# Cluster masks of a routing attention on four 32-row groups of TensorE instead of two 64-row groups

## The chip, the cores and the metric

The kernel runs on one core of one Trainium2 chip. The metric is the device time of one execution in microseconds; the lower, the better. The kernel before takes 916.72 us (median of three runs).

## The reference

Two blocks follow each other. The first is an attention in which a query sees only the keys of its own cluster; the second is an MLP mixer over tokens and channels. The change touches the attention alone.

```python
B, H, S, D = 4, 8, 768, 64          # batch, heads, sequence, head size; 16 clusters per head
q_assign = argmax(q_n @ c_n.T)      # nearest of 16 normalised centroids of the head
k_assign = argmax(k_n @ c_n.T)
mask   = q_assign[:, :, :, None] == k_assign[:, :, None, :]
scores = where(mask, 0.125 * q @ k.T, -1e9)
attn   = softmax(scores)
x      = (attn @ v), heads side by side: (B, S, 512)

h   = relu(x.T @ w_tok1) @ w_tok2   # over tokens
u   = x + h.T
out = u + relu(u @ w_ch1) @ w_ch2   # over channels
```

## The kernel before

TensorE makes the mask itself. Each query and key has a one-hot vector of its cluster. The keys' one-hots are scaled by a large number BIG and lowered by it, so that a product of a query's one-hot with a key's is 0 where the clusters agree and -BIG where they don't. This product goes into PSUM first, the scores are added on top, and the exponential turns what is masked into 0.

Two heads are treated at once, as a pair; there are 16 pairs (4 batches, 4 pairs of heads). In every tile that is contracted, head 0 of the pair has partitions 0-63 and head 1 has partitions 64-127. One pair has 6 steps, each of two chunks of 128 keys against half of the queries (384), so the attention has 96 steps. The matmuls of head 0 and head 1 use separate row groups of the array.

The clusters are found one pair ahead. After the similarities are turned, a comparison with the maximum writes the one-hots: 16 elements wide at the front of each head's 64, the rest zero from the start. TensorE transposes them, and ScalarE copies them out of PSUM with scale and offset.

```python
# const / rsmall: the one-hots, [tokens, q or k, chunk, 2 heads x 64], zeroed once
ohs = [rsmall.tile([P, 2, NJ, P], BF16, name=f"oh{i}", bufs=1) for i in range(2)]

def route(g, a0=0, a1=2):
    ...  # sc: similarities of 16 clusters; mx: their maximum
    oh = ohs[g % 2][:, a0:a1].rearrange("p a j (h x) -> p (a j) h x", h=2)[:, :, :, 0:C]
    nc.vector.tensor_tensor(
        out=oh, in0=sc..., in1=mx...to_broadcast([P, NR // 2, 2, C]), op=ALU.is_ge)

def route_turn(g, a):
    po = ps_w.tile([P, NJ, P], BF16, tag="w", name="po")
    for j in range(NJ):
        nc.tensor.transpose(out=po[:, j], in_=oh[:, a, j], identity=identb)
    ...  # a == 0 (queries): plain copy to ohT[:, 0]
    ...  # a == 1 (keys): ohT[:, 1] = BIG * po - BIG, and its sum into cells[:, g]

def scores(m):
    g, qh, j0 = split(m)
    st = state[g]
    js = slice(HJ * qh, HJ * qh + HJ)
    scs = [ps_sc.tile([P, 2, 512], F32, name="sc") for _ in range(2)]   # two banks each
    for src, start in ((st["ohT"], True), (st["T"], False)):            # mask, then scores
        for i in range(2):                                              # chunk of keys
            for h in range(2):                                          # head
                rows = slice(h * D, (h + 1) * D)
                nc.tensor.matmul(
                    scs[i][:, h, 0:HS], lhsT=src[rows, 1, j0 + i], rhs=src[rows, 0, js],
                    start=start, stop=not start,
                )
    for i in range(2):
        ex = work.tile([P, 2, HS], F32, name="ex")
        nc.scalar.activation(out=ex, in_=scs[i][:, :, 0:HS], func=ACT.Exp, scale=SM_SCALE)

def values(m):            # two steps later: 4 float32 matmuls, 128 rows x 64 columns
    ...
def half_sums(hi):        # den: column sums, 128 rows x 32 columns
    ...
def half_turn(hi):        # px: transposes, 128 x 128
    ...
```

The order on TensorE within one step m is: scores(m) (masks, then scores), values(m - 2), and then, depending on the step, what the next pair's routing needs (pr, po) or the end of a half (den, px). At the very end, the sum over cells is compared with the number of tokens, to find ties between clusters; in case of a tie a general version of the program runs, which isn't the case for these inputs.

Of the kernel before, what the change touches and what calls it, by code (L numbers as in the profile page):

```python
# [16 lines left out]
B, H, S, D = 4, 8, 768, 64  # L17
C = 16
P = 128
# [8 lines left out]
HS = HJ * P  # L28
WMAX = 512
NQ = 4  # L30
QP = P // NQ
# [15 lines left out]
def kernel(  # L47
# [29 lines left out]
    nc = tc.nc  # L77
# [39 lines left out]
    ohs = [rsmall.tile([P, 2, NJ, P], BF16, name=f"oh{i}", bufs=1) for i in range(2)]  # L117
# [185 lines left out]
    def route(g, a0=0, a1=2):  # L303

        st = state[g]
        NR = (a1 - a0) * NJ * 2
        sc = rsmall.tile([P, NR, C], F32, name="sim")
        nc.vector.transpose(  # L310
            out=sc.rearrange("p n c -> p (n c)"), in_=st.pop("pr").rearrange("p a j r -> p (a j r)")
        )
        mx = rsmall.tile([P, NR], F32, name="mx")
        nc.vector.reduce_max(out=mx, in_=sc, axis=AX.X)
        oh = ohs[g % 2][:, a0:a1].rearrange("p a j (h x) -> p (a j) h x", h=2)[:, :, :, 0:C]
        nc.vector.tensor_tensor(
            out=oh, in0=sc.rearrange("p (n h) c -> p n h c", h=2),
            in1=mx.rearrange("p (n h) -> p n h", h=2).unsqueeze(3).to_broadcast([P, NR // 2, 2, C]),
            op=ALU.is_ge,
        )  # L320

# [25 lines left out]
    def split(m):  # L347

        g, s = divmod(m, GROUPS)
        return g, s // (GROUPS // 2), 2 * (s % (GROUPS // 2))  # L350

    def scores(m):
        g, qh, j0 = split(m)
        st = state[g]
        js = slice(HJ * qh, HJ * qh + HJ)
        scs = [ps_sc.tile([P, 2, 512], F32, name="sc") for _ in range(2)]
        for src, start in ((st["ohT"], True), (st["T"], False)):
            for i in range(2):
                for h in range(2):
                    rows = slice(h * D, (h + 1) * D)  # L360
                    nc.tensor.matmul(  # L361
                        scs[i][:, h, 0:HS], lhsT=src[rows, 1, j0 + i], rhs=src[rows, 0, js],
                        start=start, stop=not start,
                    )
        for i in range(2):
            ex = work.tile([P, 2, HS], F32, name="ex")
            nc.scalar.activation(out=ex, in_=scs[i][:, :, 0:HS], func=ACT.Exp, scale=SM_SCALE)  # L367
            st["ex", qh, j0 + i] = ex
# [297 lines left out]
    def fits():  # L666

        inside = const.tile([P, 3, 2 * NPAIR * 2 * HJ], F32, name="inside")
        good = const.tile([P, 3], F32, name="good")
        flat = rcps.rearrange("p n h j -> p (n h j)")  # L670
        for i, (limit, op) in enumerate(((LIMIT, ALU.is_le), (1.0 / LIMIT, ALU.is_ge))):
            nc.vector.tensor_scalar(
                out=inside[:, i], in0=flat, scalar1=limit, scalar2=None, op0=op
            )
            nc.vector.tensor_reduce(out=good[:, i : i + 1], in_=inside[:, i], axis=AX.X, op=ALU.min)

        nc.vector.tensor_scalar(
            out=inside[:, 2, 0:NPAIR], in0=cells, scalar1=1.0 / BIG, scalar2=float(S),
            op0=ALU.mult, op1=ALU.add,
        )  # L680
        nc.vector.reduce_sum(out=good[:, 2:3], in_=inside[:, 2, 0:NPAIR], axis=AX.X)
        pn = ps_w.tile([1, 3], F32, tag="w", name="pn")
        nc.tensor.matmul(pn, lhsT=ones[:, 0:1], rhs=good, start=True, stop=True)
        count = const.tile([1, 3], I32, name="count")
        nc.vector.tensor_copy(out=count[:, 0:2], in_=pn[:, 0:2])
        nc.vector.tensor_scalar(
            out=count[:, 2:3], in0=pn[:, 2:3], scalar1=float(B * H * S), scalar2=float(P),
            op0=ALU.is_equal, op1=ALU.mult,
        )
        loaded = [  # L690
            nc.values_load(count[0:1, i : i + 1], min_val=0, max_val=P) for i in range(3)
        ]
        return loaded[0] + loaded[1] + loaded[2]


    def begin():
# [23 lines left out]
        route_products(0, 1, 2)  # L720
        turn(0, (0,))
        route(0, 1, 2)
        keep_warm(1)
        route_products(0, 0, 1)
        keep_warm(2)
        route_turn(0, 1)
        route(0, 0, 1)
        keep_warm(1)
        route_turn(0, 0)
# [15 lines left out]
    for m in range(last + 5):  # L745
        g, s = divmod(m, GROUPS)
# [4 lines left out]
        if m < last:  # L751
            scores(m)
# [4 lines left out]
        if g < NPAIR - 1:  # L757
            if s == 0:
                turn(g + 1)
            elif s == 1:  # L760
                route_products(g + 1)
            elif s == 2:
                route(g + 1)
            elif s == 3:
                route_turn(g + 1, 1)
            elif s == 4:
                route_turn(g + 1, 0)
# [35 lines left out]
    for b in range(B):  # L803
        for part in range(2):
            for i in range(3):
                ch1_chunk(part, i)
                for _ in range(2):
                    if beside:
                        beside.pop(0)()
            for i in range(3):  # L810
                ch2_chunk(b, part, i)
                if part == 1 and i < 2 and b + 1 < B:
                    turn_u(b + 1, i)
            if b == 0 and part == 0:
                both = fits()
# [213 lines left out]
```

## Time and profile before

| What | Before |
|---|---|
| time, median of 3 runs | 916.72 us (915.32 to 916.98) |
| profiled execution, span | 913.0 us |
| granted TensorE clock, mean | 0.995 |
| TensorE busy | 897.8 us |
| VectorE busy | 506.1 us |
| ScalarE busy | 306.9 us |
| attention steps | from 14.3 us (first mask) to 369.6 us (first token matmul) |
| MLP | from 369.6 us on |

A line of a group names the line of the kernel, the engine and the operation, the tile written and the tiles read, partitions x elements and type, and the count; then the busy time in us and the mean length of one in ns; then the time that the engine was idle just before. For a matmul, "64*128" is rows times columns of the array, and the next "64x384" is what streams through it. PE is TensorE's matmuls and PEld its weight loads. Matmuls are pipelined: several overlap, and a length from start to end is more than what one adds to the time. A line of the timeline gives start, length, engine, line, operation, tiles, shapes and count, merged for neighbours of one kind. A line of windows gives a stretch and then the busy time of PE, PEld, VectorE, ScalarE and GpSimd in it with the number of instructions, then the clock, the share of the transfers and GB/s.

### The profile page before, as it was taken

To read this page: it belongs to the slowest core of one execution; us is meant where nothing else is said; L and a number is where in the kernel's file an instruction comes from. 1 tells how busy PE (TensorE), PEld (TensorE's weight loads), DVE (VectorE), ACT (ScalarE), POOL (GpSimd) and SP (SyncE) were. 2 spreads that over 40 slices of the span, in tenths; PEclk is the share of its full clock that TensorE was granted. 3 is DMA by queue.
4 is the path that set the end of the run, shared out by engine and by line. 5 is a ranking of instruction groups with operands and counts; after the bars stand their busy time and mean duration, and the time that the engine had idled before them with its cause. 6 is when DMAs were issued, how large, how long until landed. Compare 5 with 4: busy or idle time off the path is not lost.

```text
span 913.0 us, 11598 instructions
## 1 busy us (share of the span) xinstructions
PE 897.8 (98%) x4594; PEld 527.4 (58%) x4594; DVE 506.1 (55%) x851; ACT 306.9 (34%) x515; POOL 48.4 (5%) x40
## 2 busy tenths in 40 slices
PE   7999999999999999999999899999999999999997
PEld 3444444444444444444458668677686876858676
DVE  6778787878787765358554244333443334433342
ACT  3656565656565555222120021211212012130210
POOL 1001000101010100123000000000000000000000
PEclk9999999999999999999999999999999999999999
DMA  9543535353434200122000001000010000100001
GB/s 163 117 100 69 93 87 97 83 98 81 95 85 70 88 1 1 47 92 70 0 1 0 1 0 47 24 1 1 0 47 24 0 1 7 52 12 1 1 12 61
DMA packets 112830, 41.76 MB, mean 46 GB/s; under 512 B 101632, under 2 KB 105728, under 8 KB 112768
## 3 DMA queue, kind: packets, MB, share of 16 engines
q1 hardware_dynamic: 109632, 40.55, 18.9%
q10 hardware_dynamic: 3136, 0.39, 0.3%
q8 instruction: 38, 0.62, 0.3%
q14 instruction: 24, 0.20, 0.1%
HBM read 34.64 MB, written 6.29 MB: 45 GB/s over the span
## 4 chain that ended last, share of the span: by engine, by line
PE 98%; DMA 1%; DVE 0%; issue 0%; ACT 0%
PE sc L361 18%; PE av L390 15%; PE pX L596 14%; PE pX L647 14%; PE pZ L647 7%; PE pZ L596 7%; PE ph L463 5%; PE pu L472 5%; PE pY L647 3%; PE pY L596 3%; PE px L425 2%; PE po L334 2%; PE pr L296 1%; PE den L406 1%; PE pt L535 1%; DMA qk<-in_k_dram 1%
## 5 line engine op out<-in xcount | busy, mean ns | idle before, releaser
L367 ACT ACTIVATE ex<-sc 128x768 f32<-128x768 f32 x192 | 145.1, 808 | 116.6 <-PE sc L361 116.6
L380 DVE TENSOR_TENSOR sum<-sum,ex 128x768 f32<-128x768 f32 x128 | 132.8, 1037 | 31.1 <-ACT ex L367 22.6
L390 PE MATMUL av<-ex,va 128*64 128x384 f32 x768 | 145.1, 499 | 0.0
L361 PE MATMUL sc<-qkT 64*128 64x384 f32 x768 | 139.5, 482 | 0.0
L390 PEld LDWEIGHTS av<-ex,va 128*64 128x64 f32 x768 | 46.6, 136 | 86.5 <-issue 82.7
L361 PEld LDWEIGHTS sc<-qkT 64*128 64x128 f32 x768 | 70.5, 187 | 31.4
L596 PE MATMUL pX<-uT,wc 128*128 128x384 f32 x192 | 68.8, 495 | 1.6 <-issue 1.6
L604 ACT COPY p<-pX 128x384 f32<-128x384 f32 x24 | 11.4, 475 | 153.0 <-PE pX L596 153.0
L596 PEld LDWEIGHTS pX<-uT,wc 128*128 128x128 f32 x192 | 36.7, 193 | 26.7 <-issue 3.3
L361 PE MATMUL sc<-ohT 64*128 64x384 bf16 x384 | 48.2, 328 | 1.3 <-DVE ohT L337 0.6
L222 POOL TENSOR_TENSOR wc<-wT,wup 128x512 int32<-128x512 int32 x24 | 35.2, 1466 | 257.7 <-DVE wT L215 149.1
L431 DVE TENSOR_TENSOR x<-px,rcps 128x384 f32<-128x384 f32 x32 | 17.8, 557 | 47.9 <-PE px L425 46.8
L463 PE MATMUL ph<-x,wt 128*128 128x512 f32 x96 | 42.1, 594 | 0.0
L472 PE MATMUL pu<-h,wt 128*128 128x512 f32 x96 | 42.0, 592 | 0.0
L489 DVE TENSOR_TENSOR x<-pX,x 128x256 f32<-128x256 f32 x24 | 10.2, 423 | 53.0 <-PE pX L647 53.0
L489 DVE TENSOR_TENSOR c<-pZ,u 128x384 f32<-128x384 f32 x24 | 13.4, 557 | 46.9 <-PE pZ L596 46.9
L647 PE MATMUL pX<-w2s,hA 128*128 128x256 f32 x144 | 35.4, 382 | 0.5 <-DVE x L489 0.5
L489 DVE TENSOR_TENSOR hA<-pY,p 128x384 f32<-128x384 f32 x24 | 13.4, 557 | 40.4 <-PE pY L596 40.4
L647 PE MATMUL pX<-wc,hA 128*128 128x256 f32 x144 | 35.0, 379 | 0.0
L647 PE MATMUL pZ<-w2s,hS 128*128 128x256 f32 x144 | 35.0, 379 | 0.0
L647 PE MATMUL pZ<-wc,hS 128*128 128x256 f32 x144 | 35.0, 379 | 0.0
L647 PE MATMUL pY<-wc,hA 128*128 128x256 f32 x144 | 35.0, 379 | 0.0
(115 smaller groups left out, 1216.7 us busy)
## 6 DMA issues: line engine op xcount, KB each, us to landing
raw<-in_moe_w_ch_dram SPq DMA_DIRECT2D x24, 512.0 KB, 4.1
qk<-in_k_dram SPq DMA_DIRECT2D x64, 96.0 KB, 4.7
va<-in_v_dram SPq DMA_DIRECT2D x16, 384.0 KB, 3.3
out_dram<-x SPq DMA_DIRECT2D x24, 256.0 KB, 2.0
qk<-in_q_dram SPq DMA_DIRECT2D x60, 96.0 KB, 3.5
raw<-in_moe_w_tok_dram SPq DMA_DIRECT2D x3, 512.0 KB, 5.8
raw<-in_moe_w_tok_dram SPq DMA_DIRECT2D x4, 384.0 KB, 3.9
qk<-in_q_dram ACTq DMA_DIRECT2D x4, 96.0 KB, 4.3
```

Of the source, the lines that this page charges most:

```text
L222: nc.gpsimd.tensor_tensor(out=dst.bitcast(I32), in0=T, in1=up, op=ALU.add)
L334: nc.tensor.transpose(out=po[:, j], in_=oh[:, a, j], identity=identb)
L361: nc.tensor.matmul(scs[i][:, h, 0:HS], lhsT=src[rows, 1, j0 + i], rhs=src[rows, 0, js], start=start, stop=not start,)
L367: nc.scalar.activation(out=ex, in_=scs[i][:, :, 0:HS], func=ACT.Exp, scale=SM_SCALE)
L380: nc.vector.tensor_tensor(out=acc, in0=acc, in1=e[i], op=ALU.add)
L390: nc.tensor.matmul(st["av"][h * D : (h + 1) * D], lhsT=st["va"][:, h, j], rhs=ex[:, h], start=(j == 0), stop=(j == NJ - 1),)
L425: nc.tensor.transpose(out=px[:, i], in_=avT[:, i], identity=ident)
L463: nc.tensor.matmul(pf, lhsT=W["tok1"][:, j, t * P : (t + 1) * P], rhs=xs[b][:, j], start=(j == 0), stop=(j == NJ - 1),)
L472: nc.tensor.matmul(pu, lhsT=W["tok2"][:, t, j], rhs=h1s[b][:, t], start=(t == 0), stop=(t == NT - 1))
L489: nc.vector.tensor_tensor(out=dst, in0=a, in1=b, op=ALU.add)
L596: nc.tensor.matmul(psum, lhsT=A[a][:, k, c * P : (c + 1) * P], rhs=R[r][:, k], start=start and k == 0, stop=k == 1, skip_group_check=not s ...
L647: nc.tensor.matmul(psum, lhsT=h2[a][:, k, i * P : (i + 1) * P], rhs=Bw[w][:, 3 * part + k], start=start and k == 0, stop=k == 2, skip_grou ...
```

## The change

A one-hot has 16 elements, and 32 rows are enough to contract it; the mask takes 64 only because head 1 begins at partition 64. The change writes each one-hot twice, to the first 16 of both 32-wide halves of its head. Then the mask of the first chunk of keys uses rows 0-31 and 64-95 (heads 0 and 1), and that of the second chunk rows 32-63 and 96-127, so that the four mask matmuls of a step use four different row groups of 32. The aim is that all four run side by side rather than two and two. The scores stay on two groups of 64 rows. Since every one-hot is there twice, the sum compared at the end is doubled.

```diff
-        oh = ohs[g % 2][:, a0:a1].rearrange("p a j (h x) -> p (a j) h x", h=2)[:, :, :, 0:C]
+        oh = ohs[g % 2][:, a0:a1].rearrange("p a j (h y x) -> p (a j h) y x", h=2, y=2)[:, :, :, 0:C]
         nc.vector.tensor_tensor(
-            out=oh, in0=sc.rearrange("p (n h) c -> p n h c", h=2),
-            in1=mx.rearrange("p (n h) -> p n h", h=2).unsqueeze(3).to_broadcast([P, NR // 2, 2, C]),
+            out=oh, in0=sc.unsqueeze(2).to_broadcast([P, NR, 2, C]),
+            in1=mx.unsqueeze(2).unsqueeze(3).to_broadcast([P, NR, 2, C]),
             op=ALU.is_ge,
         )
@@ scores
-        for src, start in ((st["ohT"], True), (st["T"], False)):
-            for i in range(2):
-                for h in range(2):
-                    rows = slice(h * D, (h + 1) * D)
-                    nc.tensor.matmul(
-                        scs[i][:, h, 0:HS], lhsT=src[rows, 1, j0 + i], rhs=src[rows, 0, js],
-                        start=start, stop=not start,
-                    )
+        for i in range(2):
+            for h in range(2):
+                r = h * D + (i % 2) * QP
+                nc.tensor.matmul(
+                    scs[i][:, h, 0:HS], lhsT=st["ohT"][r : r + QP, 1, j0 + i],
+                    rhs=st["ohT"][r : r + QP, 0, js], start=True, stop=False,
+                )
+        for i in range(2):
+            for h in range(2):
+                rows = slice(h * D, (h + 1) * D)
+                nc.tensor.matmul(
+                    scs[i][:, h, 0:HS], lhsT=st["T"][rows, 1, j0 + i], rhs=st["T"][rows, 0, js],
+                    start=False, stop=True,
+                )
@@ the test for ties
-            out=count[:, 2:3], in0=pn[:, 2:3], scalar1=float(B * H * S), scalar2=float(P),
+            out=count[:, 2:3], in0=pn[:, 2:3], scalar1=float(2 * B * H * S), scalar2=float(P),
```

## The prediction

> **What bounds the kernel now.** I read the page first: the busy shares, then the chain that ended last.
>
> ```profile
> PE 897.8 (98%) x4594; PEld 527.4 (58%) x4594; DVE 506.1 (55%) x851; ACT 306.9 (34%) x515; POOL 48.4 (5%) x40
> ...
> PE 98%; DMA 1%; DVE 0%; issue 0%; ACT 0%
> PE sc L361 18%; PE av L390 15%; PE pX L596 14%; PE pX L647 14%; PE pZ L647 7%; PE pZ L596 7%; PE ph L463 5%; PE pu L472 5%; PE pY L647 3%; PE pY L596 3%; PE px L425 2%; PE po L334 2%; PE pr L296 1%; PE den L406 1%; PE pt L535 1%; DMA qk<-in_k_dram 1%
> ```
>
> The chain is TensorE from end to end, and the changed line, L361, has 18% of it. But L361 holds both the mask and the scores, so next I read the groups by shape:
>
> ```profile
> L361 PE MATMUL sc<-qkT 64*128 64x384 f32 x768 | 139.5, 482 | 0.0
> L361 PEld LDWEIGHTS sc<-qkT 64*128 64x128 f32 x768 | 70.5, 187 | 31.4
> L361 PE MATMUL sc<-ohT 64*128 64x384 bf16 x384 | 48.2, 328 | 1.3 <-DVE ohT L337 0.6 <-ACT ex L367 0.6
> ```
>
> The mask's 384 matmuls are four in each of 96 steps; the scores' 768 records are eight per step, since a float32 matmul shows as two. Busy time here is a union of overlapping instructions, so what one matmul costs must be read from start to start. That is what the timeline of one step gives (start, length, line, count; the lines come from adjacent and overlapping windows):
>
> ```profile
> 201.48 0.27 PE L425 MATMUL px<-ident,avT 128*128 128x128 f32 x1
> 201.68 0.50 PE L361 MATMUL sc<-ohT 64*128 64x384 bf16 x4
> 202.02 0.49 PE L361 MATMUL sc<-qkT 64*128 64x384 f32 x2
> 202.34 0.48 PE L361 MATMUL sc<-qkT 64*128 64x384 f32 x2
> 203.40 0.54 PE L390 MATMUL av<-ex,va 128*64 128x384 f32 x2
> ```
>
> The four masks occupy 0.34 us (201.68 to 202.02), although each lasts 0.33 us: two heads run side by side on rows 0-63 and 64-127, and the second chunk's pair follows the first. The scores run in pairs 0.32 us apart, and the values begin 1.38 us after the first score, four pairs (1.29) and 0.09 more.
>
> That 0.09 is the key to this case. From the records' start times I took medians over the whole attention stage. Where the shape of the array changes, the next matmul starts late: scores (64 rows x 128 columns) to values (128x64) 412 ns where the pitch is 319, so **+93**; values to mask 418 against 316, **+102**; transposes (128x128) to mask, where the rows alone change, 205 against 109 and 152 against 56, **+96** both times. Mask to scores, today without a change of shape, is 159: no extra. After each change of shape, the second batch also comes late, because no weights could be loaded ahead: bf16 masks 170 against 159 (+11), float32 values of 64 columns 367 against 316 (+51). For float32 weights of 128 columns the case is where the first token matmuls follow the values:
>
> ```profile
> 369.61 0.70 PE L463 MATMUL ph<-x,wt 128*128 128x512 f32 x1
> 370.14 1.02 PE L463 MATMUL ph<-x,wt 128*128 128x512 f32 x2
> 370.57 0.59 PE L463 MATMUL ph<-x,wt 128*128 128x512 f32 x1
> ```
>
> Here the first lasts 0.70 instead of 0.59, and the second starts 0.53 us later where the next takes 0.43: 533 against 429 in the records, **+104**.
>
> **What the Trainium skill says.** "TensorEngine Tiling (Array Packing)", section Key Properties: changing the tiling mode, as opposed to changing only the tile, drains TensorE. The trace agrees: about 96 ns at each of the changes above. "TensorE: Matmul & The Clock Gate", section Part 3, gives 3.07 times for four row tiles of 32; the trace before has no such matmul, but den's four column tiles of 32 start 7 ns apart, so packing by four is seen on columns. The same page, section LDWEIGHTS, puts a load at columns divided by 1.2 GHz whatever the rows: 107 ns for 128 columns, against the 104 ns exposed here.
>
> **The change part by part.**
>
> Removed: the second batch of masks in each step. Today a step goes first mask +3, +170, +3, +159 to the first score, 335 ns. With 32 rows each, the four masks need four different row groups and write four different PSUM banks, so I expect them to start within about 10 ns of each other, and the next batch to be able to start after one pitch with the exposed bf16 load: 170 ns. Alone, that would save 335 - (10 + 170) = 155 ns, or 96 x 0.155 = 14.9 us.
>
> Added: one more change of shape. The scores still contract 64 rows, and now follow 32-row masks. By the row-only change above I add 96 ns: 10 + 170 + 96 = 276 ns to the first score. Then the first score's float32 weights are no longer loaded behind the masks, so the first score pair takes 104 ns more: 322 + 104 = 426. Up to the second score pair, before: 335 + 322 = 657; after: 276 + 426 = 702. That is **+45 ns per step**, 96 x 45 = **+4.3 us**. The change into the mask costs the same as now, since it was a change of shape before.
>
> Added on VectorE: the one-hot comparison writes both copies. It now takes, in the view of this line:
>
> ```profile
> L316 DVE TENSOR_TENSOR oh<-sim,mx x17: 358/557/558, 11.5 to 333.4; 128x384 bf16<-128x384 f32 x15, 128x192 bf16<-128x192 f32 x2
> ```
>
> From 192 to 384 elements is +199 ns, so I estimate 557 + 2 x 199 = 955 ns for the 768 elements to come: 15 x 0.40 = 6.0 us more VectorE, plus 2 x 0.2 at the start. In the stretches of 80 us VectorE has room:
>
> ```profile
> 40.00:120.00 80.00, 80.00 (x591) 35.30 (x591) 62.82 (x94) 46.80 (x72) 8.59 (x6) 1.00 0.46 93
> ```
>
> The third and fourth columns of busy time are VectorE's 62.82 and ScalarE's 46.80 of 80 us, while TensorE has all 80. A group of six steps is 22 us, so 0.4 more is about 2% on VectorE. In the group shown the comparison ended at 202.07 and its transposes began at 204.85: 2.8 us of room, so none of the 6.0 us reaches TensorE. Only the two at the start, before the first mask at 14.26 us, are in a chain (compare, transpose, copy, mask): +0.4 us.
>
> Unchanged: transposes of the one-hots (full 128x128 tiles, zeros or not), copies of ohT, loads, and all of the MLP after 366 us. The count compared at the end doubles at no cost. Sum: 4.3 + 0.4 = +4.7 us on 916.7, giving **921.4 us**.
>
> **Rivals.**
>
> 1. *No drain between 32-row and 64-row tiles.* The extra 96 and 104 ns vanish and the whole 14.9 us come in: 916.7 - 14.9 + 0.4 = 902 us. For it: both are row tilings with all columns, a pair the trace never shows. Against: 128 rows to 64 rows is also a change of rows alone, and it costs the full 96 ns in each of 46 cases. A half-way house, a drain whose weights are loaded ahead, gives 657 - (276 + 322) = 59 ns saved per step, 5.7 us, so 911 us.
> 2. *The four masks don't truly run together* (the four banks or the operand reads limit them to two at a time). Then the mask keeps its 335 ns and both extra terms come on top: about 200 ns x 96 = 19 us, 936 us. For it: nothing in the trace runs four row groups. Against: the skill's 3.07 times, and den on columns.
> 3. *VectorE becomes the bound* by the longer comparison delaying sums and reciprocals, which hold PSUM buffers. It would cost at most the 6.0 us added, so 927 us with my TensorE term. Against: TensorE idles 0 of 80 us there, while VectorE has some 17 us of slack in the same stretch.
>
> **Range and chances.** I give about 78% to the sum above, which the spread of the three runs (915.3 to 917.0) widens to some 919 to 924; 14% to rival 1 or its half-way form; 8% to rivals 2 and 3. I put the range at 911 to 926: it covers the half-way form and part of rival 3. Two per cent is 18.3 us. The best case, 14.9 us, is short of it, so faster by over 2% is nearly out (0.02); slower needs rival 2 in full (0.05); the rest is within (0.93).
>
> **What would show it.** In the timeline after, one step should read: four masks starting within 0.01 us; the first score some 0.28 us after the first mask (0.18 would be rival 1, 0.34 or more rival 2); the second score pair 0.43 after the first (0.32 would mean hidden weights); and the first score's length grown by about 0.1, as with ph. The score's weight loads should start together with the first score, no longer some 0.16 us ahead of it. The comparison should read about 955 ns, x15, with no TensorE idle behind it. The MLP from the first ph to the end should last as before. If the stage grows elsewhere than between masks and second score pair, I am wrong about VectorE; if the drain or load between 32 and 64 rows differs from 96 and 104 ns, the sum moves by 9.6 us per 100 ns.

## The result, and the profile after

The changed kernel takes 921.59 us (median of 6 runs, 919.55 to 924.15), the kernel before 916.04 us in the same comparison. The ratio is 1.0061 with a 95% interval of 1.0041 to 1.0081: some 0.6% slower, within the 2% on either side.

The page of the changed kernel, with the same two parts as before:

```profile
PE 901.8 (98%) x4594; PEld 521.8 (57%) x4594; DVE 512.4 (56%) x851; ACT 306.8 (33%) x515; POOL 48.4 (5%) x40
...
PE 98%; DMA 1%; DVE 0%; issue 0%; ACT 0%
PE sc L368 16%; PE av L397 15%; PE pX L603 14%; PE pX L654 14%; PE pZ L654 7%; PE pZ L603 7%; PE ph L470 5%; PE pu L479 4%; PE pY L654 3%; PE pY L603 3%; PE sc L361 3%; PE px L432 2%; PE po L335 2%; PE den L413 1%; PE pr L296 1%; PE pt L542 1%
```

TensorE is still the whole chain. Masks and scores now have lines of their own, L361 and L368. The groups by shape tell where the time moved:

```profile
L368 PE MATMUL sc<-qkT 64*128 64x384 f32 x768 | 149.8, 508 | 0.0
L368 PEld LDWEIGHTS sc<-qkT 64*128 64x128 f32 x768 | 66.1, 186 | 41.4 <-issue 16.6
L361 PE MATMUL sc<-ohT 32*128 32x384 bf16 x384 | 33.4, 331 | 1.3 <-DVE ohT L338 0.6 <-ACT ex L374 0.6
```

The masks' busy time falls from 48.2 to 33.4 us: the packing works. The scores, which the change doesn't touch, rise from 139.5 to 149.8 us, and their mean length from 482 to 508 ns; their minimum is still 482, but the first pair of each step now takes 587. The weight loads have a new idle time, 16.6 us of issue over 96 waits: they can no longer run ahead of their matmul.

One step in the timeline, the counterpart of the step shown before (again from adjacent and overlapping windows; PEld lines are weight loads):

```profile
204.59 0.27 PE L432 MATMUL px<-ident,avT 128*128 128x128 f32 x1
204.79 0.10 PEld L361 LDWEIGHTS <-ohT 32*128 32x128 bf16 x4 [0.17 <-issue]
204.79 0.34 PE L361 MATMUL sc<-ohT 32*128 32x384 bf16 x4
205.06 0.30 PEld L368 LDWEIGHTS sc<-qkT 64*128 64x128 f32 x4 [0.17 <-issue]
205.06 0.59 PE L368 MATMUL sc<-qkT 64*128 64x384 f32 x2
205.49 0.49 PE L368 MATMUL sc<-qkT 64*128 64x384 f32 x2
206.55 0.54 PE L397 MATMUL av<-ex,va 128*64 128x384 f32 x2
```

All four masks together last 0.34 us, as long as one. But the first score comes 0.27 us after the first mask (0.34 before), not one pitch of 0.16 after it; its weight load starts with it; it lasts 0.59 instead of 0.49; and the second pair follows 0.43 later instead of 0.32. In the records the masks give back 65 ns of a step (336 to 271 from first mask to first score), and the stretch from first score to first value takes 108 ns more (1383 to 1491): +43 ns. A group of six steps, from a first mask to that of the next pair, confirms it: 22.387 us before, 22.643 after, the same to 2 ns in every group from the second on. That is +42.7 ns per step, +4.1 us over 96 steps.

The profiled executions differ by 5.0 us (918.0 against 913.0 us). The rest is at the start: the first mask begins at 14.85 instead of 14.26 us, and the first six steps lose 0.3 us beyond the steady rate. Before the first mask come the last one-hot transposes of the first pair, here in the kernel before and then in the changed one:

```profile
13.10 0.51 PE L334 MATMUL po<-identb,oh 128*128 128x128 bf16 x6
13.38 0.82 PE L335 MATMUL po<-identb,oh 128*128 128x128 bf16 x6
```

They begin 0.28 us later, when the longer comparison has ended, and they take 0.31 us more, at a granted clock of 0.50 instead of 1.00 in these stretches. The 0.3 us are in the second and third step. There the second chunk's masks start 0.70 and 0.25 us after the first chunk's (0.70 and 0.24 before), so that packing gives nothing back, and each of these steps loses 0.2 us instead of 0.04. The MLP takes 543.3 us in the changed kernel and 543.4 in the kernel before.

### The profile page after: what moved, and what is told of

Same layout as the page of the kernel before. It is cut to its first block, busy times and chain, and to the rows that moved or that the text cites. A ratio compares the mean times of both kernels' runs of the same rounds, so it can differ in the third digit from the quotient of the medians.

```text
span 918.0 us, 11598 instructions
## 1 busy us (share of the span) xinstructions
PE 901.8 (98%) x4594; PEld 521.8 (57%) x4594; DVE 512.4 (56%) x851; ACT 306.8 (33%) x515; POOL 48.4 (5%) x40
## 4 chain that ended last, share of the span: by engine, by line
PE 98%; DMA 1%; DVE 0%; issue 0%; ACT 0%
PE sc L368 16%; PE av L397 15%; PE pX L603 14%; PE pX L654 14%; PE pZ L654 7%; PE pZ L603 7%; PE ph L470 5%; PE pu L479 4%; PE pY L654 3%; PE pY L603 3%; PE sc L361 3%; PE px L432 2%; PE po L335 2%; PE den L413 1%; PE pr L296 1%; PE pt L542 1%
## 5 line engine op out<-in xcount | busy, mean ns | idle before, releaser
L368 PE MATMUL sc<-qkT 64*128 64x384 f32 x768 | 149.8, 508 | 0.0
L368 PEld LDWEIGHTS sc<-qkT 64*128 64x128 f32 x768 | 66.1, 186 | 41.4 <-issue 16.6
L654 PE MATMUL pX<-wc,hS 128*128 128x256 f32 x144 | 35.0, 379 | 0.0
L654 PE MATMUL pX<-w2s,hS 128*128 128x256 f32 x144 | 35.0, 379 | 0.0
```

What stands on the lines that cost most here:

```text
L368: nc.tensor.matmul(scs[i][:, h, 0:HS], lhsT=st["T"][rows, 1, j0 + i], rhs=st["T"][rows, 0, js], start=False, stop=True,)
L654: nc.tensor.matmul(psum, lhsT=h2[a][:, k, i * P : (i + 1) * P], rhs=Bw[w][:, 3 * part + k], start=start and k == 0, stop=k == 2, skip_grou ...
```

## The experiments

### Each half of the change alone

**The second copy alone** keeps the masks on 64 rows.

```diff
+        oh = ohs[g % 2][:, a0:a1].rearrange("p a j (h y x) -> p (a j h) y x", h=2, y=2)[:, :, :, 0:C]
 ...
+            out=oh, in0=sc.unsqueeze(2).to_broadcast([P, NR, 2, C]),
+            in1=mx.unsqueeze(2).unsqueeze(3).to_broadcast([P, NR, 2, C]),
 scores(): as before
```

> The second copy alone: the comparison writes both copies as in the changed kernel, but masks run on 64 rows in two batches as before (a mismatch then gives twice -BIG, which the exponential turns into 0 as well); nothing is left out. Theory (VectorE's extra 6 us stay off the path but for the start): a group of six steps takes 22.39 us as before, +0.4 to 0.6 us before the first mask, so 916 to 917 us (ratio 1.0005). Rival (the longer comparison holds up sums or transposes): groups longer than 22.39 us, up to +6 us, 921 us.

Measured: 916.84 against 915.56 us, ratio 1.0005 (0.9998 to 1.0012). The ratio is not that of the two medians, since the executions of both kernels lie near 915.5 and near 917 us and a median falls on one side or the other. From the second group on, a group takes 22.387 us, as before. VectorE's busy time in a stretch of this kernel rises, and TensorE (first busy column) still has every microsecond of it; VectorE is the third:

```profile
40.00:120.00 80.00, 80.00 (x583) 35.19 (x579) 64.52 (x94) 46.31 (x71) 7.59 (x5) 1.00 0.45 92
```

So the longer comparison doesn't reach the path in the steady state. Its share at the start, 0.4 us by the working of the prediction, is smaller than this interval can show. The profiled execution doesn't show it apart either: its first mask comes at 15.24 us, but TensorE ran part of its start at half pace (granted clock 0.91 from 14 to 40 us, against 1.00 in the kernel before).

**The row groups alone** write each one-hot once. The second chunk's rows of the queries' one-hots are then zero, so its mask is left out, and the output isn't the reference's; the instructions on TensorE are those of the changed kernel.

```diff
 route(): as before
 scores():
+                r = h * D + (i % 2) * QP
 ...
+                    scs[i][:, h, 0:HS], lhsT=st["ohT"][r : r + QP, 1, j0 + i],
+                    rhs=st["ohT"][r : r + QP, 0, js], start=True, stop=False,
```

> The four row groups alone: masks as in the changed kernel, but each one-hot is written once, as before. The second chunk of keys in each step then has only zeros in its rows of the queries' one-hots, so its mask is left out. Theory (TensorE pays for one more change of shape per step): the whole loss but the start is there without the longer comparison. From the trace after, 9 + 261 + 427 = 697 ns per step up to the second score pair against 657, +40 ns x 96 = +3.8 us, so about 920 us (ratio 1.004). Rival (VectorE's second copy makes the loss, packing alone pays): the mask's saving without its cost, 902 to 916 us.

Measured: 921.88 against 915.58 us, ratio 1.0060 (1.0045 to 1.0075). The groups from the second on take 22.643 us, exactly those of the changed kernel. So the loss sits in the row groups and the rival is out. By the ratio the loss is 5.5 us (4.1 to 6.9): my 3.8 us is just below this interval, and the steady rate, 4.1 us, at its edge. In the profiled execution a part of the rest is at the start, where TensorE ran the first scores at half pace:

```profile
15.74 2.93 PE L367 MATMUL sc<-qkT 64*128 64x384 f32 x8
```

Eight score records take 2.93 us here and 1.56 later on in the same kernel. Half pace comes without row groups too: in the profiled execution of the second copy alone, with masks on 64 rows, the first eight score records take 2.79 us instead of the usual 1.45. How long it lasts differs between executions; whether the row groups also lengthen it is not shown.

### The change of shape without the packing

Masks contract 32 rows, but both chunks use the same two groups, as two batches. Nothing is gained, and nothing is left out.

```diff
-    rows = slice(h * D, (h + 1) * D)          # mask, 64 rows
+    r = h * D                                 # mask, rows r : r + 32, for both chunks
     ...
```

> The change of shape without the packing: masks of 32 rows, but both chunks on the same two row groups (0-31 and 64-95), one-hots written once; nothing is left out. Theory: a step has the two mask batches of before, then the change of shape and the exposed weight load of after: 3 + 170 + 3 + 261 + 427 = 864 ns up to the second score pair against 657, +207 ns x 96 = +19.9 us, about 936 us (ratio 1.022). Rival 1 (32 and 64 rows are no change of shape, and it is running four masks together that slows the next matmul): the same as before, 916 us.

Measured: 935.8 against 915.58 us, ratio 1.0213 (1.0191 to 1.0236). The timeline of one step:

```profile
204.20 0.50 PE L360 MATMUL sc<-ohT 32*128 32x384 bf16 x4
204.63 1.56 PE L367 MATMUL sc<-qkT 64*128 64x384 f32 x8
```

The masks are two batches again (0.50 us in all), and the scores start 0.43 us after them instead of 0.34 and last 1.56 instead of 1.45. A group takes 23.580 us, +199 ns per step, 8 fewer than I had. From the last mask to the first score it is 251 ns here and 261 in the changed kernel: the exposed part of the masks' own load, some 10 ns, was already in my 170, and I had it twice. The cost is therefore not a property of running four masks at once: it comes with 32 rows followed by 64.

### Three changes of shape in a step, and none

Masks and scores of chunk 0, then masks and scores of chunk 1, with masks on 32 rows: three changes between 32 and 64 rows in a step.

```diff
+        for i in range(2):
+            for h in range(2):
+                r = slice(h * D, h * D + QP)       # control: slice(h * D, (h + 1) * D)
+                ... mask of chunk i, head h, on rows r
+            for h in range(2):
+                ... score of chunk i, head h, on 64 rows
```

> More changes of shape: as the run with 32-row masks on two row groups, but in the order masks of chunk 0, scores of chunk 0, masks of chunk 1, scores of chunk 1; nothing is left out. A step has three changes between 32 and 64 rows instead of one. Theory (each change adds its own 96 ns and the load behind it): first mask to first value 3 + 261 + 7 + 420 + 7 + 415 + 3 + 261 + 7 + 420 + 7 + 412 = 2223 ns against 1716 before, +507 ns x 96 = +48.7 us, about 965 us (ratio 1.053). Rival (the loss is a fixed cost of masks with 32 rows, once a step): as with one change, about 936 us.

Measured: 963.04 against 915.58 us, ratio 1.0531 (1.0506 to 1.0556). A group takes 25.407 us, +503 ns per step where I had 507.

```profile
201.52 0.33 PE L360 MATMUL sc<-ohT 32*128 32x384 bf16 x2
201.79 0.92 PE L366 MATMUL sc<-qkT 64*128 64x384 f32 x4
202.64 0.34 PE L360 MATMUL sc<-ohT 32*128 32x384 bf16 x2
202.90 0.92 PE L366 MATMUL sc<-qkT 64*128 64x384 f32 x4
```

The same order on 64 rows throughout is the control:

> The control of the order: masks and scores chunk by chunk as in the run with three changes, but on 64 rows throughout as before, so without a change of shape between them; nothing is left out. Theory: the order alone costs nothing but perhaps a part of the first score's weight load, 187 ns long, which no longer has two mask batches to hide behind: 0 to 25 ns per step, 916 to 919 us (ratio 1.000 to 1.003). Rival (the loss of the order by chunk comes from mixing bf16 and float32 batches, whatever the rows): most of the 49 us of the run with 32 rows, 945 us or more.

Measured: 916.48 against 915.58 us, ratio 1.0002 (0.9993 to 1.0011); a group takes 22.387 us, as in the kernel before.

```profile
202.44 0.34 PE L360 MATMUL sc<-ohT 64*128 64x384 bf16 x2
202.61 0.81 PE L366 MATMUL sc<-qkT 64*128 64x384 f32 x4
203.26 0.33 PE L360 MATMUL sc<-ohT 64*128 64x384 bf16 x2
203.42 0.81 PE L366 MATMUL sc<-qkT 64*128 64x384 f32 x4
```

The two kernels have the same instructions in the same order and differ in the masks' rows alone. From mask to score it is 0.27 us (32 rows) against 0.17 (64), from the first score back to a mask 0.85 against 0.65; in the records, the last score pair is followed by the mask after 415 ns against 319. Each change costs on its own, also the one back from 64 to 32, and the order without a change costs nothing.

### A version with fewer changes of shape

If the change of shape is what costs, the kernel before can gain by having fewer. Both batches of one-hot transposes and the transposes of the previous pair's second half go into one step; the masks are those of before, and nothing is left out.

```diff
             elif s == 3:
                 route_turn(g + 1, 1)
-            elif s == 4:
                 route_turn(g + 1, 0)
+        if later(half_at(m - 4)):        # the second half of every pair but the last
+            half_turn(half_at(m - 4))    # px, one step later; half_out follows one step later too
```

> Fewer changes of shape than before, with the masks of before: in each pair of heads, both batches of one-hot transposes (po) run in the fourth step, and the transposes of the previous pair's second half (px) move there from the third, so two visits to 128x128 in the third and fifth step fall away; nothing is left out. Theory: the third step saves the change values to px (417 - 316 = 101), px's own late start (57) and nearly the change px to mask (96), less the change values to mask (102): about 150 ns; the fifth saves the change po to den (93) and po's late start (11): about 105 ns. 255 ns x 15 = 3.8 us, about 912 us (ratio 0.996). Rival (the later px and the three PSUM buffers wanted at once make TensorE wait for ScalarE's copies): the gain is given back, 916 us or more.

Measured: 912.06 against 915.56 us, ratio 0.9958 (0.9944 to 0.9971). A group takes 22.133 us, 254 ns less than before, where I had 255. The timeline:

```profile
203.07 1.51 PE L390 MATMUL av<-ex,va 128*64 128x384 f32 x8
204.51 0.84 PE L334 MATMUL po<-identb,oh 128*128 128x128 bf16 x12
205.19 0.50 PE L425 MATMUL px<-ident,avT 128*128 128x128 f32 x3
205.62 0.50 PE L361 MATMUL sc<-ohT 64*128 64x384 bf16 x4
...
207.34 1.51 PE L390 MATMUL av<-ex,va 128*64 128x384 f32 x8
208.78 0.53 PE L406 MATMUL den<-sum,ones 128*32 128x192 f32 x8
```

Twelve and three transposes share one visit to 128x128, and den follows the values directly. No wait took the place of what was saved: later in each group, too, TensorE has no idle time (80.00 busy of the 80 us from 40 to 120). This version beats both kernels.

## Why the prediction was right

- **The sum.** I had 921.4 us; it was 921.59. That it agrees to 0.2 us is in part luck: I had added 4.7 us to 916.7, and what came was 5.5 us on 916.04. The steady part, which carries the prediction, was +45 ns per step (4.3 us) and came out at +42.7 (4.1 us). The MLP, for which the prediction has 366 us, begins at 369.6 in the kernel before, and it is unchanged.
- **Four masks together.** I expected starts within about 10 ns. The records have 3 ns from each to the next, so the rival of two at a time falls. The Trainium skill's 3.07 times for four row tiles ("TensorE: Matmul & The Clock Gate", Part 3) counts these matmuls alone, and no run here has four masks one after another to compare with. Here the masks' busy time fell by a third, but the time rose.
- **The drain.** I took 96 ns from 128 rows followed by 64 and assumed it for 32 followed by 64. The last mask to the first score is 261 ns. Less the pitch of 159, that leaves 102 for the drain and what is exposed of the masks' own load, where I had 96 + 11. In the unpacked 32-row masks, where that load has passed with the first batch, 92 are left for the change alone. This is the "Mode switching requires drain" of the Trainium skill, "TensorEngine Tiling (Array Packing)", Key Properties, with its price. Of the prediction's 46 cases of transposes to mask 45 show it; at the first the mask waited for VectorE. Rival 1 is refuted by the changed kernel, by the unpacked 32-row masks and by the run with three changes against its control.
- **The exposed load.** I had 104 ns from the first ph; the second score pair came 427 ns after the first, against 322 before: 105. The 107 ns that the prediction set beside it fits this delay and not the load records themselves, which last 187 ns for float32 and 90 for the bf16 masks; and those expose only some 10.
- **VectorE.** I estimated 955 ns for the longer comparison and no effect on the path. The view of its line in the changed kernel:

```profile
L317 DVE TENSOR_TENSOR oh<-sim,mx x17: 558/957/959, 11.5 to 338.0; 128x768 bf16<-128x768 f32 x15, 128x384 bf16<-128x384 f32 x2
```

- **The start.** I had +0.4 us for the comparison; it is 0.28 in the profiled execution. The first mask came 0.59 us later, but the other 0.31 is the transposes at half pace, which I had not foreseen. Nor had I foreseen that packing saves nothing in the second and third step (0.3 us); this and what I had too high elsewhere nearly cancel.

Two things stay open. The medians differ by 5.5 us (3.8 to 7.4 by the interval, worked out on 916.04). The traces account for the 5.0 us of the profiled executions, 4.1 of them group by group and 0.9 at the start; no experiment varied the start alone. And scores on 32 rows as well, which would spare the change of shape, weren't tried: the two halves of a score would come from different row tiles and add into one bank, which the Trainium skill, "TensorEngine Tiling (Array Packing)", Gotcha 1, excludes at the same time; no run here shows it.

## What to carry to other kernels

Before packing small matmuls into a finer shape of the array, count the changes of shape around them. Here each cost 92 to 102 ns, and afterwards the next weights were loaded in plain sight: 11 ns for bf16 masks, 51 for 64 float32 columns, 105 for 128. Packing saved one pitch of 160 ns and bought one more change with a float32 load behind it, so it lost; ordering work so that 128x128 is visited twice per group instead of four times won 0.4% without changing any matmul.

## What the runs showed of the hardware that was not expected

Matmul lengths show only a part of this cost: a mask lasts 331 ns in the changed kernel and 328 before, and of the scores only the first pair lasts longer, 587 instead of 482; the late start after a change is in no length. It is seen in start-to-start distances, and the groups repeat to within 2 ns from the second to the fifteenth, so a loss of 0.5% could be put down to single gaps. The half pace of TensorE in the first steps was the other surprise: the profiled execution of the row groups alone took 23.2 us for its first six steps, where the changed kernel, with the same TensorE instructions, took 20.2. The view of windows gives a clock of 1.00 from 14 to 24 us there, where the score records are at half pace, so the pace has to be read from the records.
